# Expert products of a mixture layer: Strassen's seven products over pairs of hidden tiles and pairs of token blocks

## The chip, the cores and the metric

One core of one Trainium2 chip runs the whole program. The metric is device time in microseconds (us) of one execution. A core has TensorE (matmuls into eight PSUM banks of 128 x 512 floats), ScalarE (ACT), VectorE (DVE), GpSimd (POOL) and 16 DMA engines; SP issues most transfers. Each engine takes its instructions in the order in which they stand, and waits for others by semaphores.

## What is computed

Three layers, one after another. The middle one is a mixture of eight experts in which every token goes through every expert, weighted by a gate matrix P that Sinkhorn rounds balance:

```python
x = attention(q, k, v, beta)                 # 3072 tokens x 384
P = exp(x @ w_gate - max)                    # 3072 x 8
for _ in range(8):
    P /= P.sum(1, keepdims=True) + 1e-09
    P /= P.sum(0, keepdims=True) + 1e-09
    P *= N / E
for e in range(E):                           # E = 8, hidden size 1024
    h = np.maximum(x @ w1[e], 0.0)
    out += P[:, e:e + 1] * (h @ w2[e])
h = out @ w_in                               # hidden size 2048
return (h * np.cos(h)) @ w_out
```

## The kernel before, in words

Every operand of a matmul is kept as two parts, `hi` (its leading bits) and `lo` (the remainder), so that a product of two numbers is three matmuls: hi x hi, hi x lo, lo x hi. A token block is 512 tokens (there are six), a hidden tile 128 columns of `w1[e]` (eight per expert), and the model dimension 384 is three tiles of 128 (`KD = 3`). The first product of a hidden tile and a block is thus 3 x 3 = 9 matmuls of 128x128 by 128x512 (`h_mms`, line 132), followed by ReLU and split: ScalarE writes `hi` (line 159), VectorE the remainder `lo` (line 160). The second product is 9 matmuls into three banks (`yT_mms`, line 153), which sum over the expert's eight hidden tiles.

The program has these stages. While attention runs, expert 0 is worked through block by block in its gaps (`moe0_h`, `moe0_y`; `half()` takes the next piece); its results go to DRAM (`ysc`). The blocks of tokens, split, go to DRAM too (`xsc`). When attention's memory is closed, `begin_blocks` (line 802) loads all six blocks and six accumulators into SBUF, where they stay; expert 0's last block, the Sinkhorn rounds (`sk_some`, lines 583 to 621) and the first weights overlap. Then a single loop over experts 1 to 7, blocks and hidden tiles (line 1156) issues the first product of the next step, then the second product of this one. Once per expert and block, `moe_acc` multiplies the three banks by the gate (VectorE, line 1021) and adds them to the accumulator (GpSimd, line 1022). Weights are loaded once per expert, two hidden tiles at a time, and split by ScalarE and VectorE (`w_half`, lines 122 and 123). In the same loop, pieces of `conv` (lines 933 to 968) turn the 64-bit weights of the last layer into two floats on VectorE. `net_step` and `net_y` are the last layer; a rounding step of it (line 1064) and the splitting of its inputs are GpSimd's, as is the issuing of its weight loads (`w2_load`, lines 1043 and 1044).

```python
for i, (e, b, f) in enumerate(steps):
    if i + 1 < len(steps):
        moe_h(i + 1)
    ...
    moe_y(i)
    ...
    n = i // FT
    if n and 1 <= f <= 3:
        moe_acc(n - 1, f - 1)
```

Of the kernel before, what the change touches and what calls it, by code (L numbers as in the profile page):

```python
# [35 lines left out]
def kernel(  # L36
# [544 lines left out]

    def sk_max():
        nc.vector.tensor_reduce(out=mx, in_=logits.rearrange("p u e -> p (u e)"), axis=AX.X, op=ALU.max)

    def sk_max_t():
        nc.tensor.transpose(pa[3][0:1, 0:128], mx, ident)
        nc.vector.tensor_reduce(out=mr, in_=pa[3][0:1, 0:128], axis=AX.X, op=ALU.max)

    def sk_exp():
        nc.tensor.matmul(out=pa[3][:, 128:129], lhsT=ones[0:1, :], rhs=mr, start=True, stop=True)  # L590
        nc.vector.tensor_scalar(out=neg_mx, in0=pa[3][:, 128:129], scalar1=-1.0, scalar2=None, op0=ALU.mult)
        nc.scalar.activation(out=P, in_=logits, func=ACTF.Exp, bias=neg_mx)
        sk_rows()
# [17 lines left out]
    def sk_T():  # L611
# [29 lines left out]
    def moe0_y(s):  # L641
# [3 lines left out]
        if f == FT - 1:  # L645
            for kd in range(KD):
                if m in acc:
                    nc.scalar.activation(out=acc[m][:, kd, :], in_=yb[kd], func=ACTF.Copy)
                else:
                    y = ap2.tile([128, 512], F32, tag="y0", name="y0")  # L650
                    nc.scalar.activation(out=y, in_=yb[kd], func=ACTF.Copy)
                    nc.sync.dma_start(out=ysc[m][:, kd, :], in_=y)
                    stored.add(m)
# [8 lines left out]
    with tc.manual_schedule():  # L662
# [129 lines left out]
        xblk, xq, bigp, scr = {}, [], [], []  # L792

        def x_tile():
            return bigp[0].tile([128, 2, KD, 512], F32R, tag="x", name="x", bufs=NB)

        def load_block(b):
            nc.gpsimd.dma_start(out=xblk[b], in_=xsc[b])
            if b in stored:
                nc.sync.dma_start(out=acc[b], in_=ysc[b])  # L800

        def begin_blocks():

            att.close()
            bigp.append(ctx.enter_context(tc.tile_pool(name="big", bufs=1)))
            for b in range(NB):
                xblk[b] = x_tile()
            for b in range(NB):
                acc[b] = bigp[0].tile([128, KD, 512], F32, name=f"acc{b}")
            scr.append(hp.tile([128, 3072], F32, tag="xb", name="scr"))  # L810
            stage.append(scr[0][:, 1536:3072])

            w_load(NG + 1, scr[0][:, 0:1536])
            w_load(NG + 2)
            load_block(0)
            xq.extend(lambda b=b: load_block(b) for b in range(1, NB))

# [432 lines left out]
```

## Time and profile before

| what | value |
|---|---|
| median of 3 runs | 2257.78 us (2255.49 to 2258.95) |
| span of the profiled execution | 2254.0 us |
| TensorE busy | 2194.1 us |
| VectorE, ScalarE, GpSimd busy | 977.0, 627.2, 513.2 us |
| moved by DMA | 123.93 MB |

The profile is of one execution: from its first to its last instruction are 2254.0 us, 3.78 us less than the median of the runs, which is timed around the whole of it; the profile gives no other time for that execution. A busy engine may still wait inside an instruction: a matmul's time is from its start to its result, and matmuls follow each other faster than that, so their pace is read from the distance of their starts. PE stands for TensorE, PEld for its weight loads, "PEclk" for the share of full clock that it was granted. `<-` names what released an engine that had been idle.

### The profile page before, as it was taken

The numbers are of one execution on the slowest core, as the hardware profiler recorded it, in microseconds if no ns is written. First come the engines' busy times: TensorE is split into PE (matmuls) and PEld (weight loads), VectorE is DVE, ScalarE is ACT, GpSimd is POOL, SyncE is SP. The second block draws the span as 40 slices with busy tenths as digits, with TensorE's granted clock in tenths as the row PEclk, the third lists the DMA queues.
The fourth block names the chain that finished last, engine by engine and source line by source line (L and its number), as shares of the span: only waits on it lengthen the run. The fifth ranks groups of instructions, "written<-read, shape, count | busy, mean of one in ns | idle before, by whom it ended". The sixth has DMA issues, their size and how long they took to land.

```text
span 2254.0 us, 38564 instructions
## 1 busy us (share of the span) xinstructions
PE 2194.1 (97%) x16693; PEld 1837.2 (82%) x16693; DVE 977.0 (43%) x1591; ACT 627.2 (28%) x1017; POOL 513.2 (23%) x717
## 2 busy tenths in 40 slices
PE   6889999999999999999999999999999999999998
PEld 5677777788888888888888888888888878888887
DVE  6554543352343344334333433433322236666665
ACT  2233332321121122112112211211111135566665
POOL 4656544302210110111011101101111122222221
PEclk7889999999999999999999999999999999999999
DMA  4442321433131012112202210210112130000000
GB/s 83 101 94 66 80 66 52 180 102 104 44 84 47 26 49 80 28 30 80 52 23 58 70 32 26 80 52 27 43 37 65 38 113 2 14 15 15 15 15 15
DMA packets 167723, 123.93 MB, mean 55 GB/s; under 512 B 80272, under 2 KB 159664, under 8 KB 166784
## 3 DMA queue, kind: packets, MB, share of 16 engines
q1 hardware_dynamic: 161904, 97.26, 16.0%
q0 software_dynamic: 4480, 23.90, 3.1%
q8 instruction: 131, 2.15, 0.4%
q10 hardware_dynamic: 1168, 0.30, 0.1%
q14 instruction: 40, 0.33, 0.0%
HBM read 90.65 MB, written 30.77 MB: 54 GB/s over the span
## 4 chain that ended last, share of the span: by engine, by line
PE 92%; DVE 4%; ACT 2%; issue 1%; POOL 1%; DMA 0%; DVEq 0%; POOLq 0%; ACTq 0%
PE ps L132 43%; PE ps L153 34%; PE ps L142 8%; PE ps L281 1%; PE ps L467 1%; PE ps L255 1%; PE ps L437 1%; PE ps L449 1%; PE ps L495 1%; PE ps L510 0%; PE ps L542 0%; PE ps L525 0%; POOL kr L210 0%; DVE kr L246 0%; DVE xb L548 0%
## 5 line engine op out<-in xcount | busy, mean ns | idle before, releaser
L132 PE MATMUL ps<-x,w1t 128*128 128x512 f32 x3564 | 874.4, 390 | 0.0
L153 PE MATMUL ps<-h,w2t 128*128 128x512 f32 x3456 | 854.4, 392 | 0.0
L132 PEld LDWEIGHTS ps<-x,w1t 128*128 128x128 f32 x3564 | 668.0, 188 | 136.2
L153 PEld LDWEIGHTS ps<-h,w2t 128*128 128x128 f32 x3456 | 648.3, 189 | 135.1
L160 DVE SCALAR_TENSOR_TENSOR h<-ps,h 128x512 fp32r<-128x512 f32 x384 | 265.5, 691 | 945.4 <-ACT h L159 945.4
L159 ACT ACTIVATE h<-ps 128x512 fp32r<-128x512 f32 x384 | 229.5, 598 | 1229.9 <-PE ps L132 1229.9
L1022 POOL TENSOR_TENSOR acc<-acc,scr 128x512 f32<-128x512 f32 x126 | 166.1, 1318 | 1098.5 <-DVE scr L1021 1092.5
L142 PE MATMUL ps<-w2t,h 128*128 128x384 f32 x720 | 138.1, 338 | 5.0 <-DVE h L1088 2.1
L142 PEld LDWEIGHTS ps<-w2t,h 128*128 128x128 f32 x720 | 126.9, 188 | 14.5 <-DVE h L1088 4.5
L1078 DVE TENSOR_TENSOR tp<-tp,ps 128x512 f32<-128x512 f32 x96 | 66.0, 688 | 146.1 <-ACT tp L1077 146.1
L132 PE MATMUL ps<-xb,w1t 128*128 128x512 f32 x432 | 115.3, 410 | 6.1 <-ACT xb L547 2.7
L1064 POOL TENSOR_SCALAR tp<-tp 128x512 f32<-128x512 f32 x96 | 60.0, 625 | 256.5 <-ACT tp L1063 256.3
L132 PEld LDWEIGHTS ps<-xb,w1t 128*128 128x128 f32 x432 | 79.4, 192 | 26.4 <-DVE xb L548 3.5
L360 POOL TENSOR_TENSOR w1t<-w1t 128x30 f32<-128x30 f32 (+9 forms) x180 | 96.3, 535 | 14.1
L356 POOL TENSOR_TENSOR w1t<-Nsys,w1t 128x30 f32<-128x30 f32 (+9 forms) x180 | 90.4, 502 | 13.6
L1021 DVE TENSOR_TENSOR scr<-ps,scr 128x512 f32<-128x512 f32 x126 | 85.9, 682 | 8.6 <-DMA scr<-pts 5.6
L142 PE MATMUL ps<-x,h 128*128 128x384 f32 x432 | 83.5, 339 | 0.0
L1083 ACT ACTIVATE h<-tp 128x512 fp32r<-128x512 f32 x96 | 60.7, 632 | 76.9 <-DVE tp L1078 70.2
L132 PE MATMUL ps<-x 128*128 128x512 f32 x324 | 80.8, 393 | 1.3 <-DVE scr L1021 1.3
L1072 ACT ACTIVATE tp<-tp 128x512 f32<-128x512 f32 x96 | 60.7, 632 | 73.2 <-DVE tp L1069 73.2
L142 PEld LDWEIGHTS ps<-x,h 128*128 128x128 f32 x432 | 76.2, 188 | 5.7 <-DVE h L1088 2.5
L132 PEld LDWEIGHTS ps<-x 128*128 128x128 f32 x324 | 60.2, 188 | 12.7 <-DVE scr L1021 1.6
(187 smaller groups left out, 1411.0 us busy)
## 6 DMA issues: line engine op xcount, KB each, us to landing
scr<-in_moe_w_dram SPq DMA_DIRECT2D x54, 384.0 KB
scr<-pts SPq DMA_DIRECT2D x48, 256.0 KB
xsc<-xb SPq DMA_DIRECT2D x24, 384.0 KB
x<-xsc POOLq DMA_DIRECT2D x6, 1536.0 KB, 10.3
tp<-in_moe_w_in_dram SPq DMA_DIRECT2D x16, 384.0 KB
wsa<-tp SPq DMA_DIRECT2D x32, 192.0 KB
tp<-in_moe_w_out_dram SPq DMA_DIRECT2D x16, 384.0 KB
wsb<-tp SPq DMA_DIRECT2D x32, 192.0 KB
```

Source lines behind the costliest of these rows:

```text
L132: nc.tensor.matmul(out=ps[:, :nn], lhsT=w[:, a, kk, fs], rhs=x[:, b, kk, c0:c0 + nn], start=(i == 0), stop=(i == 3 * KD - 1),)
L142: nc.tensor.matmul(out=ps[:, :DM], lhsT=h[:, a, ts], rhs=w[:, b, f % 2, :], start=(first and i == 0), stop=(last and i == 2),)
L153: nc.tensor.matmul(out=banks[kd], lhsT=w[:, a, f % 2, kd * 128:(kd + 1) * 128], rhs=h[:, b, :], start=(first and b == 0 and a == 0), stop= ...
L159: nc.scalar.activation(out=h[:, 0, :nn], in_=ps[:, :nn], func=ACTF.Relu)
L160: nc.vector.scalar_tensor_tensor(out=h[:, 1, :nn], in0=ps[:, :nn], scalar=0.0, in1=h[:, 0, :nn].bitcast(F32), op0=ALU.max, op1=ALU.subtract,)
L356: eng.tensor_tensor(out=a, in0=nsys[:, j + 1:, j:j + 1].to_broadcast([128, n, j]), in1=xsys[:, j:j + 1, 0:j].to_broadcast([128, n, j]), op ...
L360: eng.tensor_tensor(out=xsys[:, j + 1:, 0:j], in0=xsys[:, j + 1:, 0:j], in1=a, op=ALU.add)
L1021: nc.vector.tensor_tensor(out=t, in0=ysets[n % 2][kd], in1=pb[e, b], op=ALU.mult)
L1022: nc.gpsimd.tensor_tensor(out=acc[b][:, kd, :], in0=acc[b][:, kd, :], in1=t, op=ALU.add)
L1072: nc.scalar.activation(out=rr[i % 2], in_=rr[i % 2], func=ACTF.Abs)
L1078: nc.vector.tensor_tensor(out=c, in0=c, in1=hb2(i), op=ALU.mult)
L1083: nc.scalar.activation(out=h[:, 0], in_=c, func=ACTF.Copy)
```

## The change

For experts 1 to 7 the loop is turned round: pairs of token blocks are the outer loop (three), then experts, then groups of two hidden tiles (four), 84 groups in all. In a group the first product is a 2 x 2 by 2 x 2 matrix of tiles (two model tiles by two hidden tiles, times two model tiles by two blocks), and is made by seven products of sums of tiles in the form of Strassen and Winograd, each of three matmuls. The third model tile is done so that its two cross terms (hi x lo and lo x hi, the smaller ones scaled by 4096) ride along as a fourth matmul in each of the seven (`c` and `T[:, 2, :]`), and its hi x hi is four single matmuls (`zz`). The results are put together in four PSUM banks (A, G, B, D) by copies from bank to bank on ScalarE and two additions on VectorE. Sums of tokens (`t_prep`) are made once per pair, kept in SBUF as `T0` to `T6`, and those of pairs 1 and 2 are written to DRAM (`tsc`) in the background and loaded at the change of pair. Sums of weights (`s_prep`) are made in every group, by GpSimd from the raw weights, which are loaded anew for each pair. The second product of two groups and one block is four pieces of nine matmuls (`seg_piece`), put between the seven products as fill (`F`); after four pieces the banks go through the gate (`gates`), twice per expert and block instead of once. Only two accumulators are in SBUF; finished ones go to DRAM (`xacc`) and come back for the last layer.

```diff
-        steps = [(e, b, f) for e in range(1, E) for b in range(NB) for f in range(FT)]
...
+        def mm(bank, n, i, start=False, stop=True):
+            h, l, c = s_hi(n, i), s_lo(n, i), s_c(n, i)
+            T = Tt[i]
+            for q, (a, b) in enumerate(((h, T[:, 0, :]), (h, T[:, 1, :]), (l, T[:, 0, :]), (c, T[:, 2, :]))):
+                nc.tensor.matmul(
+                    out=bank, lhsT=a, rhs=b, start=start and q == 0, stop=stop and q == 3, skip_group_check=True
+                )
+
+        def zz(bank, n, f, t):
+            nc.tensor.matmul(
+                out=bank, lhsT=s_z(n, f), rhs=Tt[(1, 6)[t]][:, 2, :], start=False, stop=True, skip_group_check=True
+            )
...
+        def seg_piece(m, q):
+
+            n = m // 2 * 2 + q // 2
+            h = hm_t.pop((n, q % 2, m % 2))
+            w2_t[-1] = W2[n]
+            yT_mms(yb, -1, q % 2, h, q == 0, q == 3)
+            if q == 3:
+                gq.append(m)
...
+        def gates():
+            while gq:
...
+                for kd in range(KD):
+                    c = ctile()
+                    nc.vector.tensor_tensor(out=c, in0=yb[kd], in1=pslot[t], op=ALU.mult)
+                    nc.gpsimd.tensor_tensor(out=accp[t][:, kd, :], in0=accp[t][:, kd, :], in1=c, op=ALU.add)
+                if j >= NG - 2:
+                    if e + 1 < E:
+                        p_load(t, e + 1, b)
+                    else:
+                        nc.sync.dma_start(out=xacc[b], in_=accp[t])
+                        if p + 1 < NP:
+                            acc_begin(p + 1, t)
+                            late.append(lambda p=p, t=t: acc_mul(p + 1, t))
...
+            s7, s4 = ctile(), ctile()
+            mm(A_, n, 0, True)
+            tl(0)
+            mm(G_, n, 5, True)
+            tl(5)
+            copy(B_, A_)
+            F()
+            gates()
+            if n >= 2:
+                fill.extend([lambda m=n - 2, q=q: seg_piece(m, q) for q in range(4)])
+            copy(s7, G_)
+            nx[0]()
+            mm(A_, n, 4)
+            tl(4)
+            copy(D_, A_)
+            mm(B_, n, 1)
+            zz(B_, n, 0, 0)
+            zz(G_, n, 1, 1)
+            skp(n)
+            nx[1]()
+            bg()
+            F()
+            mm(D_, n, 3)
+            tl(3)
+            mm(A_, n, 2)
+            zz(A_, n, 1, 0)
+            tl(2)
+            tl(1)
+            copy(s4, D_)
+            skp(n)
+            relu(n, 0, 0, B_)
+            nc.vector.tensor_tensor(out=s7, in0=A_, in1=s7, op=ALU.add)
+            nx[2]()
+            nx[3]()
+            nx[4]()
+            while late:
+                late.pop(0)()
+            F()
+            mm(D_, n, 6)
+            zz(D_, n, 0, 1)
+            tl(6)
+            skp(n)
+            nc.vector.tensor_tensor(out=s4, in0=G_, in1=s4, op=ALU.add)
+            relu(n, 1, 0, s7)
+            bg()
+            nx[5]()
+            if n + 2 < NGR:
+                g_load(n + 2)
+            relu(n, 1, 1, s4)
+            F()
+            relu(n, 0, 1, D_)
+            bg()
...
+        lead = [tq[0], tq[1], sq[0], tq[2], sq[1], sq[2], tq[3], sq[3], tq[4], sq[4], tq[5], sq[5], tq[6], tq[7]]
+        nb = 0
+        while len(mq) > 4:
+            half()
+            nb += 1
+            for _ in range(2):
+                if lead:
+                    lead.pop(0)()
+            if nb % 2 == 0:
+                sk_some()
+        for x in lead:
+            x()
+        g_load(1)
```

`nx` are the six pieces of `s_prep` for the next group: four sums on GpSimd, splits on ScalarE and VectorE, four more sums on GpSimd, and the split of `w2`. `bg` takes a piece of background work: first the token sums of pairs 1 and 2, then `conv`. `tl` loads the next pair's tiles in the last group of a pair, `skp` does one Sinkhorn round in groups 0 to 2, and `acc_mul` weights the reloaded sum of expert 0 by its gate. `tq` are the eight pieces of the token sums of the first pair, which stand beside what is left of expert 0 (`mq`).

**Order, TensorE in the middle of experts 1 to 7.** Before, one row is nine matmuls:

```order
L153 MATMUL ps8_98<-h_11448,w2t_10204 128x512 x9
L132 MATMUL ps8_98<-x_6345,w1t_11102 128x512 x9
L153 MATMUL ps8_98<-h_11471,w2t_11103 128x512 x9
L132 MATMUL ps8_98<-x_6345,w1t_11154 128x512 x9
L153 MATMUL ps8_98<-h_11494,w2t_11103 128x512 x9
L132 MATMUL ps8_98<-x_6345,w1t_11154 128x512 x9
```

In the change, most of one group; `T_6348` to `T_6354` are `T0` to `T6`, `mh` are hidden tiles, line 1179 is `mm`, 1184 `zz`, 155 the second product:

```order
L1179 MATMUL ps_107<-T_6348,w1t 128x512 x4
L1179 MATMUL ps_107<-T_6353,w1t 128x512 x4
L155 MATMUL ps_107<-mh,w2t 128x512 x9
L1179 MATMUL ps_107<-T_6352,w1t 128x512 x4
L1179 MATMUL ps_107<-T_6349,w1t 128x512 x4
L1184 MATMUL ps_107<-T_6349,w1t 128x512
L1184 MATMUL ps_107<-T_6354,w1t 128x512
L155 MATMUL ps_107<-mh,w2t 128x512 x9
L1179 MATMUL ps_107<-T_6351,w1t 128x512 x4
L1179 MATMUL ps_107<-T_6350,w1t 128x512 x4
L1184 MATMUL ps_107<-T_6349,w1t 128x512
L155 MATMUL ps_107<-mh,w2t 128x512 x9
```

First and second product no longer alternate nine by nine; not shown of this group are product 6 (four), its single matmul and a fourth nine of line 155; with them it is 32 matmuls of the first product and 36 of the second.

**Order, VectorE in the same place.** Before, a ReLU's remainder now and then stands beside conversion (lines 955 to 962) and gate products:

```order
L160 SCALAR_TENSOR_TENSOR h<-ps_98,h 128x512
L960 TENSOR_SCALAR tp<-tp 128x384
L961 SCALAR_TENSOR_TENSOR tp<-tp 128x384
L962 SCALAR_TENSOR_TENSOR tp<-tp 128x384
L160 SCALAR_TENSOR_TENSOR h<-ps_98,h 128x512 x2
L1021 TENSOR_TENSOR scr<-ps_98,scr 128x512
```

In the change, from the first hidden tile's remainder (line 162) on: the two sums of banks (1306 and 1317), the weights of the next group (976 to 989, and 1004) and conversion (1150 to 1152) stand in one row:

```order
L162 SCALAR_TENSOR_TENSOR mh<-ps_107,mh 128x512
L1306 TENSOR_TENSOR ct<-ps_107,ct 128x512
L976 TENSOR_TENSOR w1t<-scr,w1t 128x128
L977 TENSOR_TENSOR w1t<-scr,w1t 128x256
L981 SCALAR_TENSOR_TENSOR w1t<-scr,w1t 128x256
L989 TENSOR_TENSOR w1t<-ct,w1t 128x512
L1317 TENSOR_TENSOR ct<-ps_107,ct 128x512
L162 SCALAR_TENSOR_TENSOR mh<-ct,mh 128x512
L1150 TENSOR_SCALAR tp<-tp 128x384
L1151 SCALAR_TENSOR_TENSOR tp<-tp 128x384
L1152 SCALAR_TENSOR_TENSOR tp<-tp 128x384
L1004 TENSOR_TENSOR w2t<-scr,w2t 128x768
```

Work that was spread over four steps now stands between the end of one product and the next gate products.

**Order, ScalarE at the end of attention**, with what each waits for. Before (159 is ReLU of expert 0, 122 the weights, 592 the exponential of the gates):

```order
L122 ACTIVATE w1t<-stg 128x768 [waits Pool_49]
L122 ACTIVATE w2t<-stg 128x768 [waits Activation_49]
L159 ACTIVATE h<-ps_98 128x512 [waits DVE_49,PE_49] x2
L122 ACTIVATE w1t<-scr 128x768 [waits DMAHW6_49]
L122 ACTIVATE w2t<-scr 128x768 [waits DMAHW7_49]
L592 ACT_TABLE_LOAD [waits DVE_49]
L592 ACTIVATE P<-logits,small 128x192 [waits Activation_49]
L159 ACTIVATE h<-ps_98 128x512 [waits PE_49,Activation_49] x2
```

In the change, the splits of token sums (1034, 1082) and the sums of weights (965 to 988, 1003) stand between the ReLUs (161):

```order
L161 ACTIVATE h<-ps_107 128x512 [waits DVE_49,PE_49]
L1034 ACTIVATE T_6351<-mh 128x512 [waits DVE_49]
L965 ACTIVATE w1t<-scr 128x128 [waits DMAHW4_49,Pool_49]
L966 ACTIVATE w1t<-scr 128x256
L968 ACTIVATE w1t<-scr 128x256
L969 ACTIVATE w1t<-w1t 128x256 [waits Activation_49]
L161 ACTIVATE h<-ps_107 128x512 [waits PE_49]
L1034 ACTIVATE T_6353<-mh 128x512 [waits DVE_49]
L988 ACTIVATE w1t<-ct 128x512 [waits Pool_49]
L1034 ACTIVATE T_6352<-mh 128x512 [waits DVE_49]
L161 ACTIVATE h<-ps_107 128x512 [waits PE_49]
L1034 ACTIVATE T_6350<-mh 128x512 [waits DVE_49]
```

The ReLUs of expert 0's last block, on which TensorE waits, now stand behind instructions that wait for VectorE, GpSimd and DMA.

## Rows read from the trace of the kernel before

**Rows 1.** The page: busy us, share of the span and instructions of each engine.

```profile
PE 2194.1 (97%) x16693; PEld 1837.2 (82%) x16693; DVE 977.0 (43%) x1591; ACT 627.2 (28%) x1017; POOL 513.2 (23%) x717
```

**Rows 2.** Busy time by stretch; columns PE, PEld, DVE, ACT, POOL, then PEclk, DMA share, GB/s.

```profile
560.00:1792.00 1232.00, 1232.00 (x5437) 1020.15 (x5436) 444.80 (x744) 215.90 (x351) 169.68 (x128) 1.00 0.17 49
```

**Rows 3.** Timeline of two steps: start us, us, instruction [idle before <- releaser].

```profile
1001.45 2.20 PE L153 MATMUL ps<-h,w2t 128*128 128x512 f32 x9
...
1001.64 0.60 ACT L159 ACTIVATE h<-ps 128x512 fp32r<-128x512 f32 x1 [3.48 <-PE ps L132]
...
1002.27 0.69 DVE L160 SCALAR_TENSOR_TENSOR h<-ps,h 128x512 fp32r<-128x512 f32 x1 [2.79 <-ACT h L159]
...
1003.49 2.20 PE L132 MATMUL ps<-x,w1t 128*128 128x512 f32 x9
```

**Rows 4.** Groups of instructions with shapes: busy us, mean ns, idle before.

```profile
L1022 POOL TENSOR_TENSOR acc<-acc,scr 128x512 f32<-128x512 f32 x126 | 166.1, 1318 | 1098.5 <-DVE scr L1021 1092.5 <-issue 6.0
...
L1021 DVE TENSOR_TENSOR scr<-ps,scr 128x512 f32<-128x512 f32 x126 | 85.9, 682 | 8.6 <-DMA scr<-pts 5.6 <-POOL acc L1022 2.8
...
L123 DVE TENSOR_TENSOR w1t<-scr,w1t 128x768 fp32r<-128x768 f32 x27 | 25.8, 957 | 1.9 <-ACT w1t L122 1.1
...
L952 DVE SCALAR_TENSOR_TENSOR tp<-tp 128x384 f32<-128x384 f32 x32 | 17.9, 559 | 1.1
...
L957 DVE TENSOR_SCALAR tp<-tp 128x384 int32<-128x384 int32 x32 | 11.5, 360 | 1.1
...
L356 POOL TENSOR_TENSOR w1t<-Nsys,w1t 128x130 f32<-128x130 f32 x12 | 5.2, 431 | 0.9
```

**Rows 5.** Timeline at 640 us: VectorE and GpSimd.

```profile
640.36 0.95 DVE L123 TENSOR_TENSOR w1t<-scr,w1t 128x768 fp32r<-128x768 f32 x1
...
640.52 1.93 POOL L1022 TENSOR_TENSOR acc<-acc,scr 128x512 f32<-128x512 f32 x1 [2.73 <-DVE scr L1021]
...
641.23 2.04 DVE L123 TENSOR_TENSOR w2t<-scr,w2t 128x768 fp32r<-128x768 f32 x1
```

**Rows 6.** Timeline and TensorE's waits, expert 0's last block.

```profile
429.14 0.39 SPq L105 DMA_DIRECT2D scr<-in_moe_w_dram  x1
...
436.49 2.33 PE L132 MATMUL ps<-xb,w1t 128*128 128x512 f32 x9
...
446.31 0.15 DVE L604 TENSOR_SCALAR small<-ps 128x8 f32<-128x8 f32 x1
...
448.67 0.53 DVE L600 TENSOR_REDUCE small<-P 128x8 f32<-128x192 f32 x1
...
PE ps L603 <- DVE small L600: 0.3, 1, 0.3
```

**Rows 7.** Busy time by stretch, while blocks are loaded; the last column is GB/s.

```profile
430.00:432.00 2.00, 2.00 (x11) 1.68 (x11) 1.23 (x2) 1.67 (x3) 0.00 (x0) 1.00 0.91 284
...
440.00:442.00 2.00, 2.00 (x10) 1.43 (x9) 1.96 (x4) 0.92 (x2) 0.00 (x0) 1.00 1.08 436
```

**Rows 8.** Busy time by stretch around a pause of TensorE.

```profile
308.00:312.00 4.00, 2.83 (x13) 1.80 (x11) 2.57 (x2) 1.11 (x3) 0.00 (x0) 1.00 0.30 112
312.00:316.00 4.00, 4.00 (x138) 3.78 (x139) 3.41 (x3) 1.31 (x4) 0.89 (x1) 0.92 0.19 70
316.00:320.00 4.00, 4.00 (x68) 2.96 (x69) 0.00 (x0) 1.13 (x2) 3.31 (x11) 0.66 0.51 97
```

**Rows 9.** Timeline of TensorE and GpSimd at the turn to the net.

```profile
1841.34 1.51 PE L142 MATMUL ps<-w2t,h 128*128 128x384 f32 x7 [0.65 <-DVE h L1088]
...
1844.03 0.80 PE L142 MATMUL ps<-w2t,h 128*128 128x384 f32 x3 [1.18 <-DVE scr L1021]
...
1846.11 2.35 PE L132 MATMUL ps<-x 128*128 128x512 f32 x9 [1.28 <-DVE scr L1021]
...
1850.12 2.00 PE L142 MATMUL ps<-w2t,h 128*128 128x384 f32 x10 [1.32 <-DVE h L1088]
...
1812.71 0.55 POOL L1043 DMA_DIRECT2D w1t<-wsa  x1
```

More of the change, by code (lines that the diff above doesn't have):

```diff
@@ L627, in sk_some @@
             sk.pop(0)()
-    h0_t, acc, stored = {}, {}, set()
+    h0_t, tmp2 = {}, [lambda: ap2.tile([128, 512], F32, tag="y0", name="y0")]
     def moe0_h(s):
         m, f = divmod(s, FT)
-        bank = pa[0] if scr and s % 2 else hb
+        bank = pa[0] if scr and s % 2 and not grp else hb
         h_mms(bank, f // 2, f, xb[m], 0, 512)
@@ L646, in moe0_y @@
             for kd in range(KD):
[L647 to L653, printed above, removed]
+                y = tmp2[-1]()
+                nc.scalar.activation(out=y, in_=yb[kd], func=ACTF.Copy)
+                nc.sync.dma_start(out=ysc[m][:, kd, :], in_=y)
     NS0 = NB * FT
@@ L789 @@
         nc.scalar.activation(out=wg[:, :, 0, :], in_=wg_sb, func=ACTF.Copy)
[L792 to L816, printed above, removed]
+        scr, grp = [], []
         mq = [(2, lambda: moe0_h(0))]
@@ new lines, with F, bg, skp @@
+        fill = []
+        def F():
+            if fill:
+                fill.pop(0)()
+        bgq = []
+        def bg(k=1):
+            for _ in range(k):
+                if bgq:
+                    bgq.pop(0)()
+        def skp(n):
+            if n <= 2 and sk:
+                sk_some()
+                if not sk:
+                    for t in range(2):
+                        acc_begin(0, t)
+                        late.append(lambda t=t: acc_mul(0, t))
+        def group(n):
+            p, e, j = gidx(n)
+            swap = e == E - 1 and j == NG - 1 and p + 1 < NP
+            nx = s_prep(n + 1) if n + 1 < NGR else [lambda: None] * 6
+            def tl(i):
+                if swap:
+                    t_load(p + 1, i)
+            s7, s4 = ctile(), ctile()
[50 more added lines that the diff above has]
+            bg()
@@ L1207 @@
-        w2_load(7)
-        for kd in (0, 2, 1):
-            moe_acc(len(steps) // FT - 1, kd)
+        grp.append(1)
+        skb[0] = hb
+        for bank in (B_, D_):
+            nc.tensor.matmul(
+                out=bank, lhsT=s_hi(0, 0), rhs=Tt[0][:, 0, :], start=True, stop=True, skip_group_check=True
+            )
+        fill.extend(lambda: half() for _ in range(len(mq)))
+        group(0)
+        assert not fill and not mq
+        tpv = tpt.rearrange("p a (s c) -> p (a s) c", c=512)
```

374 lines of the change are left out of this document (263 added, 111 removed).

## The prediction

> **What bounds the kernel now.** I read the page's busy times first: TensorE is busy 97% of the span, twice any other engine [rows 1]. I then cut the span by stage. In the stage of experts 1 to 7 the engine has no idle time at all: 1232.00 of 1232.00 us busy at clock 1.00 [rows 2]. So this stage is worth what its matmuls take, one after another, and nothing else. Their pace comes from the timeline: nine matmuls of the second product start at 1001.45, the next nine at 1003.49 [rows 3]: 2.04 us for nine, 0.2267 us each (the 0.39 us that the profile gives one matmul is its latency, not its pace). The 336 steps of 18 matmuls make 6048 x 0.2267 = 1371 us, from about 448 to 1811 us. The other engines have slack: per step of 4.08 us ScalarE works 0.60 and waits 3.48, VectorE 0.69 and mostly waits [rows 3].
>
> **What the change takes away.** One group (two hidden tiles, two token blocks) had 2 x 2 x 9 = 36 matmuls in the first product. Now it has seven products of four, and four single ones: 32. The second product keeps its 36. All are 128x128 by 128x512 as before, so I price them at the same pace. There are 7 experts x 4 x 3 pairs = 84 groups: 84 x 4 x 0.2267 = **76.2 us less**. Two added matmuls that only prime banks cost 0.5 us.
>
> **One group laid out in time.** The 68 matmuls take 15.4 us if nothing waits. From the order of the change: product 0 ends at 0.9, product 5 at 1.8, nine of the second product (I call nine such a filler) at 3.85, then products 4 and 1 and two single ones to 6.1, filler to 8.2, products 3 and 2 and a single to 10.2, filler to 12.2, product 6 and a single to 13.4, filler to 15.4. Results are readable some 0.2 us later.
> ScalarE (0.60 us each for 512 columns [rows 4]; a copy from bank to bank has no row, and I take the same; its bounds are 0.4 and 1.2, and neither reaches a wait): copy A to B at 1.1, needed at 4.8; copy of G at 2.0, needed at 5.9; copy A to D at 4.95, needed at 8.2; four weight pieces to 7.1; copy of D at 9.3, needed at 12.2. Every one is 2 us early or more.
> GpSimd: three gate additions of 1.32, then eight weight sums of 128x128. The nearest row is 128x130, 0.43 [rows 4]: 4.0 + 3.4 = 7.4 of 15.4 us.
> VectorE is the tight one. It makes three gate products of 0.68 [rows 4] from 4.05 to 6.1; TensorE's next filler overwrites their banks one by one from 6.1 on. Then it waits behind ScalarE's copy of D and the first ReLU until 10.5. From there in order: remainder of the first hidden tile 0.69 [rows 3], sum 0.68, three weight remainders (my estimate 1.15 in all, scaled from 0.96 for 768 columns [rows 4]), one of 512 columns 0.69, sum 0.68, remainder 0.69, weights of the second product 0.96, two remainders 1.38: it ends at 17.4. In every second group three conversion operations (0.56 twice and 0.36 [rows 4]) make it 18.9. The next gate products can start at 15.4 + 3.85 + 0.2 = 19.4, and TensorE wants the first of them at 15.4 + 6.1 = 21.5, so the chain may end at 20.8: 1.9 us to spare with a conversion, 3.4 without.
> What eats into that is seen at 640 us [rows 5]: GpSimd's addition, started during VectorE's 0.95 us subtraction of two SBUF tiles, took 1.93 instead of 1.29, and VectorE's next one, started under it, 2.04 instead of 0.95. The second to start waits for the first. The change puts five such VectorE operations and four GpSimd sums in the same 4 us. Taking turns with pieces of 0.43 puts 0.8 to 1.7 on VectorE's chain: with a conversion it ends at 19.7 to 20.6. Still before 20.8, by little; without one, 1.7 to 2.6 us are left.
> [...]
> **Steady term: +8 us**, 0 to 20. About 4 for the sums of tokens of pairs 1 and 2, which sit on ScalarE, VectorE and GpSimd beside groups 2 to 11, some ten pieces of which push a bank copy past its time by about 0.4; 4 for conversion groups at the edge. Below nothing it can't be.
>
> **Weights and tokens by DMA.** Weights are now read and split three times (84 loads of 768 KB, 66 MB for 22). One takes 786 KB / 284 GB/s = 2.8 us [rows 7], and I allow 5 for issue and landing. It is issued when VectorE has read the old ones (13 to 16.5) and first needed 5.5 us into the next group (20.9), and 4 us later than that ScalarE's delay would reach product 6. Hidden by the matmuls; each microsecond beyond would be one per group. At the two changes of pair 5.5 MB of token tiles go through: at 436 GB/s [rows 7] 13 us, at 284 19. Tile 1 is issued at 10.3 and wanted at 20.2, tile 6 at 13.4 and 21.3. I take **+1 us**, 0 to 10. The store and reload of the two accumulators holds up SP and GpSimd, so the next weights land 9 us into a group; product 6's cover of 12.2 holds.
>
> **The start** is where the gain goes. Before, expert 0's last block (420 to 463 us) ran beside weight splits and the Sinkhorn rounds, and TensorE's matmuls waited 0.3 us for those [rows 6]. Now the token sums for the first pair stand there too, on ScalarE ahead of the ReLUs and on VectorE ahead of the maximum, on whose transpose TensorE waits in order. I walked the order with the rows' durations:
> - 3.7 MB are queued ahead of the first sum. They can start at 429 as the weights do now [rows 6], and at 284 to 436 GB/s [rows 7] land near 439; two additions of 1.32, subtraction, copy, remainder, and the maximum is out at 443. TensorE has run out at 438.4, nine matmuls later than those of 436.49 start [rows 6]: **4.7**, then **1.0** at the next small matmul.
> - the first Sinkhorn round waits for two more sums, the weights of group 0, the table load: **5.5**; the next stands behind four corrections of 0.69: **3.0**, and 0.5 inside group 0.
> - group 1 has no filler yet (32 matmuls, 7.3 us), while VectorE has some 10 us of its own and up to three Sinkhorn rounds of 2.9 [rows 6]: product 5 waits 4.0 for a bank, product 4 2.7 for ScalarE, 2.6 more: **9.3**. Group 2 in the same way **4.2**.
> Sum **+28 us**. Bounds: the 0.3 of before, and 45 if nothing of it overlaps.
> Pauses also cost clock: the row from 308 has TensorE idle 1.2 us, and in the next 8 us the granted clock is 0.92 and 0.66, a mix of 1.2 and 2.4 GHz [rows 8]: (0.08 + 0.34) x 4 = 1.7 us lost. Some eight pauses above 1 us would lose 14; part falls into time that is waited anyway. **+6 us**, 2 to 14.
>
> **The end.** Before, TensorE idles 4.4 us at the turn to the last net [rows 9]. Now the last accumulator must be stored before GpSimd may issue the load into its place, and ten issues of 0.55 [rows 9] stand ahead of the third rounding step: additions 5.0, store 4, issues 5.5, against 11 us of ready matmuls. I get 8 us idle: **+4 us**, 0 to 8. The net itself keeps its order and its pace.
>
> **Sum:** -76.2 + 0.5 + 28 + 6 + 4 + 8 + 1 = -28.7. The profiled span of 2254.0 becomes 2225.3; the median of the runs shown is 3.8 above that span, and so **2229 us**. A measurement of this kernel can tell about 0.2% (4.5 us) from no change.
>
> **Rivals.**
> 1. *The start overlaps better.* The transfers land at 400 GB/s and more [rows 7], the pauses shrink to 12 and their clock to 3: 2229 - 19 = **2210**. For: DMA did 436 just there. Against: in-order queues.
> 2. *Conversion groups overrun.* If each GpSimd sum also waits its full turn, VectorE ends 0.5 us too late in some 40 groups: 20 us: **2249**. For: [rows 5]. Against: the chain still has 0.2 to 1.1 us left. The part above 2253 I count as same.
> 3. *Slower: VectorE becomes the bound of every group.* Its chain from 10.5 needs only 3 us more than I have, from waiting its turn at every operation with two SBUF inputs and from hand-overs between engines. From 0.35 us of TensorE wait per group on the gain is gone (29 / 84). One us each is 84 - 8 more: **2305**. Against: plain groups keep some 2 us. For: no stretch of the profile runs VectorE and GpSimd this densely on each other's tiles.
> 4. *The matmuls are not saved*: they are counted in the order, so I give it nothing.
>
> **How the numbers follow.** Forecast 0.55 (2213 to 2245), rival 1 0.17, rival 2 0.16 (0.10 faster, 0.06 same), rival 3 0.12. Faster 0.55 + 0.17 + 0.10 = 0.82, same 0.06, slower 0.12. Range: below, start and end at their low bounds, about 2198; above, start, clock and steady terms high, 2260. It leaves out rival 3.
>
> **What would show it.** Right: in the middle of the stage 68 matmuls per 15.4 us with TensorE busy throughout; idle TensorE of some 28 us between 436 and 505, waiting for VectorE in lines of the Sinkhorn matmuls and of groups 1 and 2; the granted clock below 1 there; a gap of about 8 us at the turn to the net. Wrong: TensorE waits for VectorE's gate products in every group; subtractions of 512 columns at 1 us and more in the mean; bank copies late; the weights' DMA named as a releaser.

## The result, and the profile after

The change made the kernel 1.0% slower: median 2282.38 us of 4 runs (2277.26 to 2283.63) against 2258.36 us, ratio 1.0101 (95% interval 1.0086 to 1.0115). The forecast was 2229 us, faster than before. The profiled execution has a span of 2279.6 us. The page's busy times, as in [rows 1]:

```profile
PE 2170.4 (95%) x16359; PEld 1787.7 (78%) x16359; DVE 1439.6 (63%) x2285; ACT 994.4 (44%) x1819; POOL 1090.8 (48%) x1521
```

TensorE works 24 us less than before and yet the span is 26 us longer. Where that is, busy time by stretch shows (columns as in [rows 2]; the x behind a busy time counts instructions, matmuls in the first column). After: expert 0's last block and groups 0 to 4, groups 5 to 29, the first change of pair, groups 33 to 57, the second change with the groups around it, groups up to the last, last group and net:

```profile
419.95:566.82 146.87, 115.12 (x452) 88.03 (x450) 85.58 (x168) 52.11 (x103) 53.31 (x64) 0.90 0.39 130
566.82:961.83 395.01, 394.60 (x1702) 319.06 (x1700) 281.83 (x447) 184.78 (x362) 225.70 (x280) 1.00 0.37 116
961.83:1019.38 57.55, 50.78 (x206) 40.35 (x205) 34.08 (x54) 21.34 (x42) 32.66 (x35) 0.94 0.39 128
1019.38:1413.71 394.33, 394.33 (x1702) 319.19 (x1700) 289.38 (x466) 179.28 (x350) 218.12 (x276) 1.00 0.32 99
1413.71:1482.86 69.15, 65.51 (x273) 51.61 (x272) 48.76 (x75) 28.53 (x56) 41.76 (x46) 0.98 0.36 117
1482.86:1814.10 331.24, 331.24 (x1429) 268.09 (x1428) 223.10 (x360) 149.88 (x294) 182.42 (x231) 1.00 0.25 77
1814.10:2279.57 465.47, 442.63 (x2166) 391.82 (x2164) 268.25 (x418) 253.04 (x423) 110.84 (x150) 0.98 0.15 51
```

Before, the two stretches that stand beside the first and the last of these:

```profile
419.45:560.00 140.55, 138.72 (x620) 112.41 (x618) 58.80 (x132) 33.12 (x54) 21.43 (x15) 1.00 0.42 148
...
1792.00:2254.00 462.00, 449.27 (x2201) 396.87 (x2200) 265.98 (x413) 252.52 (x422) 95.13 (x132) 1.00 0.08 25
```

Three things are to be seen. **The groups run without a gap**, as forecast: 394.33 of 394.33 us busy at clock 1.00. But a stretch of 394.33 us holds 1702 matmuls, 0.2317 us each, where [rows 2] give 1232.00 / 5437 = 0.2266. **The start** takes 146.87 us for 452 matmuls, 35 of them the small ones of gates and Sinkhorn rounds, at clock 0.90; 417 x 0.2267 = 94.5 are 52.3 us short of it. Before, 140.55 us hold 620, also 35 small: 7.9 short. So the start lost 44.4 us. **The changes of pair** and **the end** have pauses: 57.55 - 50.78 = 6.8 us at the first change, 69.15 - 65.51 = 3.6 at the second, both with the clock below 1 behind them. The end is 3.5 us longer than before with 35 matmuls fewer (7.9 us): 11.4 us lost.

What TensorE waited for, over the whole span (us in total, times, longest):

```profile
PE ps L144 <- DVE h L1391: 14.9, 1, 14.9
...
PE ps L1179 <- ACT ct L1189: 12.1, 4, 3.5
PE ps L590 <- DVE small L587: 8.7, 1, 8.7
PE ps L607 <- DVE small L604: 5.8, 4, 3.3
PE ps L155 <- DVE ct L1233: 5.0, 3, 3.7
```

And in the timeline of a group, beside [rows 3]:

```profile
704.13 2.24 PE L155 MATMUL ps<-mh,w2t 128*128 128x512 f32 x9
706.21 1.10 PE L1179 MATMUL ps<-T,w1t 128*128 128x512 f32 x4
```

Nine of the second product now start 2.08 us before the next matmul (704.13 to 706.21), where [rows 3] have 2.04. Nothing is named as a releaser: a pause of a few ns inside every matmul has no row of its own.

| term of the sum | forecast, us | measured, us |
|---|---|---|
| 336 matmuls fewer, two more | -75.7 | -75.7 |
| pace of the groups: 84 x (15.77 - 15.41) | 0 | +30 |
| start, with its clock (44.4 less 1.8 of pace) | +34 | +43 |
| sums and conversion inside groups | +8 | +1 |
| changes of pair, with their clock | +1 | +16 |
| end (11.4 less one group's pace) | +4 | +11 |
| sum; the span moved by +25.6 | -28.7 | +25 |

15.77 us is the distance of one group's first matmul to the next one's, the same for 72 of the 83 distances to 0.01 us. The pair term is what five groups at the two changes took beyond 15.77 us each (5.3, 4.9, 4.3, 1.7 and 0.1 us).

### The profile page after: what moved, and what is told of

It reads as the page before. It is cut to its first block, busy times and chain, and to the rows that moved or that the text cites. A ratio compares the mean times of both kernels' runs of the same rounds, so it can differ in the third digit from the quotient of the medians.

```text
span 2279.6 us, 40883 instructions
## 1 busy us (share of the span) xinstructions
PE 2170.4 (95%) x16359; PEld 1787.7 (78%) x16359; DVE 1439.6 (63%) x2285; ACT 994.4 (44%) x1819; POOL 1090.8 (48%) x1521
## 4 chain that ended last, share of the span: by engine, by line
PE 85%; DVE 5%; DMA 4%; ACT 2%; issue 2%; POOL 2%; SPq 1%; POOLq 0%; DVEq 0%; ACTq 0%
PE ps L155 32%; PE ps L1179 22%; PE ps L134 12%; PE ps L144 8%; PE ps L1184 3%; PE ps L283 1%; PE ps L257 1%; DMA accp<-ysc 1%; PE ps L469 1%; DMA xacc<-accp 1%; DMA scr<-in_moe_w_dram 1%; PE ps L451 1%; PE ps L439 1%; POOL accp L1234 1%; POOL accp L1220 1%
## 5 line engine op out<-in xcount | busy, mean ns | idle before, releaser
L155 PE MATMUL ps<-mh,w2t 128*128 128x512 f32 x3024 | 754.1, 394 | 5.0 <-DVE ct L1233 5.0
L155 PEld LDWEIGHTS ps<-mh,w2t 128*128 128x128 f32 x3024 | 569.7, 189 | 140.3 <-DVE ct L1233 7.5
L1179 PE MATMUL ps<-T,w1t 128*128 128x512 f32 x2352 | 613.4, 400 | 21.5 <-ACT ct L1189 12.1
L1179 PEld LDWEIGHTS ps<-T,w1t 128*128 128x128 f32 x2352 | 445.0, 190 | 130.5 <-ACT ct L1189 14.2
L1234 POOL TENSOR_TENSOR accp<-accp,ct 128x512 f32<-128x512 f32 x252 | 334.9, 1356 | 326.6 <-DVE ct L1233 326.6
L162 DVE SCALAR_TENSOR_TENSOR mh<-ps,mh 128x512 fp32r<-128x512 f32 x168 | 115.1, 685 | 311.8 <-ACT mh L161 311.8
L1189 ACT ACTIVATE ps<-ps 128x512 f32<-128x512 f32 x168 | 97.8, 582 | 324.7 <-PE ps L1179 313.9
L1233 DVE TENSOR_TENSOR ct<-ps,scr 128x512 f32<-128x512 f32 x252 | 158.3, 683 | 76.4 <-PE ps L155 73.7
L1189 ACT ACTIVATE ct<-ps 128x512 f32<-128x512 f32 x168 | 100.3, 597 | 219.7 <-PE ps L1179 214.3
L161 ACT ACTIVATE mh<-ct 128x512 fp32r<-128x512 f32 x168 | 106.2, 633 | 131.6 <-DVE ct L1306 71.2
L144 PE MATMUL ps<-w2t,h 128*128 128x384 f32 x720 | 138.6, 340 | 16.5 <-DVE h L1391 14.9
L162 DVE SCALAR_TENSOR_TENSOR mh<-ct,mh 128x512 fp32r<-128x512 f32 x168 | 144.1, 858 | 0.1
L1184 PE MATMUL ps<-T,w1t 128*128 128x512 f32 x336 | 119.8, 397 | 0.0
L155 PE MATMUL ps<-h,w2t 128*128 128x512 f32 x432 | 117.8, 420 | 0.0
```

Source lines behind the costliest of these rows:

```text
L144: nc.tensor.matmul(out=ps[:, :DM], lhsT=h[:, a, ts], rhs=w[:, b, f % 2, :], start=(first and i == 0), stop=(last and i == 2),)
L155: nc.tensor.matmul(out=banks[kd], lhsT=w[:, a, f % 2, kd * 128:(kd + 1) * 128], rhs=h[:, b, :], start=(first and b == 0 and a == 0), stop= ...
L161: nc.scalar.activation(out=h[:, 0, :nn], in_=ps[:, :nn], func=ACTF.Relu)
L162: nc.vector.scalar_tensor_tensor(out=h[:, 1, :nn], in0=ps[:, :nn], scalar=0.0, in1=h[:, 0, :nn].bitcast(F32), op0=ALU.max, op1=ALU.subtract,)
L1179: nc.tensor.matmul(out=bank, lhsT=a, rhs=b, start=start and q == 0, stop=stop and q == 3, skip_group_check=True)
L1184: nc.tensor.matmul(out=bank, lhsT=s_z(n, f), rhs=Tt[(1, 6)[t]][:, 2, :], start=False, stop=True, skip_group_check=True)
```

## The experiments

Theories at the outset: the pace is lost to the **addresses** of the token tiles, or (rival) to the **density** of the other engines' accesses; the pauses come from what stands ahead in **in-order queues**, or (rival) from the **transfers and work** themselves, in any order.

### The pace: where the tiles start

The allocator puts `T0` to `T6` at the upper end of SBUF; `T0` starts at byte 186,336 of each partition, 32 past a multiple of 64. All operands of the large matmuls before (`x`, `h`, weights) start at multiples of 64. These addresses stand in no row of a trace; they are read from the built programs. Experiment 1 adds 32 bytes to that pool, so that `T0` starts at byte 186,304, a multiple of 64, and to that of the net, whose weights lay the same way:

```diff
         Tt = [tpool.tile([128, 3, 512], F32R, name=f"T{i}") for i in range(7)]
+        tpool.tile([128, 8], F32, name="pad")
```

> Theory (address): the token tiles T0 to T6 start 32 bytes past a multiple of 64, every tile that TensorE streamed before at a multiple of 64, and this costs some of each matmul's pace. With 32 bytes more in the pool all tiles lie at multiples of 64: a group should fall from 15.77 us to 15.41 (68 x 0.2267), 84 x 0.36 = 30 us less, about 2252 us (2247 to 2257). Rival (density: the many reads and writes of the other engines slow the matmuls): nothing changes, 15.77 us per group and 2278 to 2286 us.

Measured: 2254.16 us, ratio to before 0.9983 (0.9974 to 0.9992). Experiments 2 and 8 go the other way, in the kernel before: `x` moved by 32 bytes, then the weights alone (the second tile brings what lies behind back to a multiple of 64).

```diff
+            bigp[0].tile([128, 8], F32, name="pad")
             for b in range(NB):
                 xblk[b] = x_tile()
+            bigp[0].tile([128, 8], F32, name="pad2")
...
     hp = ctx.enter_context(tc.tile_pool(name="hp", bufs=2))
+    wp.tile([128, 8], F32, tag="pad", name="pad", bufs=1)
+    hp.tile([128, 8], F32, tag="pad", name="pad2", bufs=1)
```

> The kernel before, with only its blocks of tokens moved by 32 bytes. Theory (address): 9 of the 18 matmuls of a step read such a tile. The changed kernel lost 0.36 us in 68 matmuls of which 32 do; in proportion a step of 4.08 us grows by about 0.1, 336 steps by some 33 us: about 2291 us (2275 to 2305). Rival (density): the other engines do the same as before, so no change, 2254 to 2262 us.

> The kernel before, with only its weight tiles moved by 32 bytes (read by TensorE as the stationary operand, and as the streamed one in 720 matmuls of the last layer); tokens and hidden tiles stay. If only the streamed operand's address counts: no change beyond some 3 us in the last layer, 2254 to 2264 us. If the stationary one counts as much: 33 us and more, 2285 to 2330 us.

Measured: 2288.03 us, ratio 1.0133 (1.0118 to 1.0148), and 2299.97 us, 1.0181 (1.0166 to 1.0196). The duration of a matmul of line 1179 (first product) and 155 (second) between 1019 and 1414 us, as min/median/max in ns; first the changed kernel:

```profile
L1179 PE MATMUL ps<-T,w1t x700: 393/397/400, 1019.4 to 1411.2; 128*128 128x512 f32 x175
...
L155 PE MATMUL ps<-mh,w2t x901: 387/393/403, 1019.1 to 1413.5; 128*128 128x512 f32 x181
```

Experiment 1 (its line 1180 is `mm`; the maxima are matmuls right behind a pause that ends at 1411 us, at its second change of pair), and its busy time by stretch:

```profile
L1180 PE MATMUL ps<-T,w1t x706: 388/390/794, 1019.1 to 1412.3; 128*128 128x512 f32 x177
...
L155 PE MATMUL ps<-mh,w2t x911: 388/390/629, 1019.8 to 1413.6; 128*128 128x512 f32 x183
```

```profile
1020.00:1400.00 380.00, 380.00 (x1678) 314.85 (x1677) 285.96 (x461) 176.57 (x344) 213.73 (x270) 1.00 0.32 102
```

380.00 us hold 1678 matmuls: 0.2265 us each, the old pace with all the new density around it. Experiment 2 (line 132 first, 153 second product) and, in the stretch of [rows 2], experiments 2 and 8:

```profile
L132 PE MATMUL ps<-x,w1t x846: 392/396/400, 1021.1 to 1411.7; 128*128 128x512 f32 x170
...
L153 PE MATMUL ps<-h,w2t x853: 388/394/398, 1019.2 to 1413.5; 128*128 128x512 f32 x171
```

```profile
560.00:1792.00 1232.00, 1232.00 (x5307) 997.22 (x5306) 441.32 (x737) 210.68 (x342) 163.85 (x122) 1.00 0.17 48
```

```profile
560.00:1792.00 1232.00, 1232.00 (x5281) 989.67 (x5280) 438.51 (x738) 210.25 (x341) 160.53 (x119) 1.00 0.16 47
```

With 5437 in the same 1232.00 us before, the pace went from 0.2266 to 0.2321 and 0.2333 us, while the other engines did what they had always done. So the address decides, in both kernels and for the streamed and the stationary operand alike. The second product was slowed in experiment 2 too (394), though its own tiles had not moved: it alternates with matmuls that were slowed. How a delay passes on was not tried; nor were offsets other than 32.

### The changes of pair

> The changed kernel with one transfer issue (the gate row of expert 1, which waits for GpSimd's weighting of the reloaded accumulator) moved behind the weights of the next group in the queue. Theory (queue): at both changes of pair TensorE waits because the weights are issued behind that wait; 16 us were lost at the two changes, 3 should stay: about 2269 us (2264 to 2274), and no pause of over 1 us at the changes. Rival (transfers: 5.5 MB at each change take the time that they take): the pauses stay, 2278 to 2286 us.

```diff
-            p_load(t, 1, b)
+            late2.append(lambda t=t, b=b: p_load(t, 1, b))
...
                 g_load(n + 2)
+            while late2:
+                late2.pop(0)()
```

Measured: 2276.73 us, 1.0079 (1.0064 to 1.0095), a gain of under 6 us where 13 were expected. The queue in the changed kernel, first SP's timeline, then ScalarE's:

```profile
954.78 0.34 SPq L1239 DMA_DIRECT2D xacc<-accp  x1
...
958.60 0.33 SPq L1216 DMA_DIRECT2D accp<-ysc  x1
968.12 0.36 SPq L1208 DMA_DIRECT2D scr<-pts  x1
...
969.66 0.48 SPq L924 DMA_DIRECT2D scr<-in_moe_w_dram  x1
...
976.07 0.31 ACT L965 ACTIVATE w1t<-scr 128x128 fp32r<-128x128 f32 x1 [8.57 <-DMA scr<-in_moe_w_dram]
...
977.34 0.58 ACT L1189 ACTIVATE ct<-ps 128x512 f32<-128x512 f32 x1
```

SP loads the new accumulator at 958.60, then stands until 968.12, when GpSimd has weighted it, for the gate row; only then come the weights (969.66). They reach ScalarE at 976.07. Its copy of bank D, due in this group, stands behind them in its queue (977.34), and that is the row `L1179 <- ACT ct L1189`. In experiment 3 the longest pauses at the two changes fell to 1.4 and 1.2 us, as the theory had it, but one elsewhere grew, in group 3:

```profile
PE ps L155 <- DVE ct L1233: 15.4, 1, 15.4
```

The edit had moved the row for the first pair too, where group 3 needs it at once (3.7 us there before). Experiment 6 moves it for pairs 1 and 2 alone (`if p:` ahead of the new line, the old one else), on top of experiment 5:

> The one before, with the gate row of expert 1 issued behind the next group's weights, for pairs 1 and 2 alone (the third experiment had moved it for pair 0 too). Theory (queue): the two changes of pair lose 16 us, of which 3 stay: 13 us less than the one before, about 2230 us (2225 to 2235). Rival (transfers): under 4 us less than the one before.

Measured: 2245.35 us, 0.9937 (0.9921 to 0.9954), 12.4 us less than experiment 5. At the first change TensorE then waits 0.3 us for a token tile, and this:

```profile
PE ps L1181 <- DVE ct L1322: 1.3, 1, 1.3
```

### The end

> The changed kernel with the last layer's weight loads issued by SP instead of GpSimd. Theory (queue): GpSimd's rounding step stands behind ten issues that wait for the store of the accumulator; without them it runs at 1859.4 instead of 1872.4, TensorE's pause of 15 us becomes about 2, and of the 13.7 us at half clock behind it most goes: about 2266 us (2261 to 2271). Rival (weights late): the pause moves to the first hidden tile whose weights are loaded there and less than 5 us are gained, 2277 to 2285 us.

```diff
-            nc.gpsimd.dma_start(out=a, in_=wsa[g])
-            nc.gpsimd.dma_start(out=c, in_=wsb[g])
+            nc.sync.dma_start(out=a.bitcast(F32), in_=wsa[g])
+            nc.sync.dma_start(out=c.bitcast(F32), in_=wsb[g])
```

Measured: 2283.02 us, 1.0113 (1.0096 to 1.0130): no gain. GpSimd in the changed kernel, its last additions, the first of ten issues, and the rounding step:

```profile
1855.61 3.79 POOL L1234 TENSOR_TENSOR accp<-accp,ct 128x512 f32<-128x512 f32 x3 [4.74 <-DVE ct L1233]
1864.06 0.57 POOL L1346 DMA_DIRECT2D xw<-wsa  x1 [4.66 <-DMA xacc<-accp]
...
1872.38 0.63 POOL L1367 TENSOR_SCALAR tp<-tp 128x512 f32<-128x512 f32 x1
```

The issues stand from 1859.4 to 1872.4 ahead of the rounding: 4.7 us until the accumulator is stored, ten issues of 0.55, and 2.9 us ahead of the ninth and the tenth. In experiment 4 that pause is down to 1.9 us, but a new one takes its place (TensorE's waits, then ScalarE's timeline):

```profile
PE ps L144 <- ACT h L1386: 12.8, 1, 12.8
```

```profile
1883.40 0.63 ACT L1332 ACTIVATE xx<-nacc 128x512 fp32r<-128x512 f32 x1 [14.02 <-DMA nacc<-xacc]
```

The next accumulator's load had stood ahead of the weights on SP and now stood behind 7.9 MB of them (ten loads of 768 KB). Experiment 7 puts it first again, on top of experiment 6:

```diff
+        x2_load(1)
         for g in range(3, 8):
             w2_load(g)
-        x2_load(1)
```

> The one before, with the last layer's weight loads on SP's queue and the load of the second accumulator ahead of them (in the fourth experiment it stood behind them, and TensorE waited 13 us for it). Theory (queue order): the pause of 15 us falls to about 2 and of its 13.7 us at half clock most goes: 14 us less than the one before, about 2216 us (2210 to 2222). Rival (transfers): 7.7 MB of weights are late in any order, the pause moves again, under 5 us less than the one before.

Measured: 2229.60 us, 0.9875 (0.9859 to 0.9891), 15.8 us less than experiment 6, and 29 us less than the kernel before in the same runs. TensorE's wait at this place:

```profile
PE ps L144 <- DVE h L1398: 1.9, 1, 1.9
```

### The start

Line 587 is the maximum whose transpose TensorE awaits. In the changed kernel it ran at 447.36, behind a token sum that waited for GpSimd, which waited for a load (GpSimd, then VectorE):

```profile
442.06 1.26 POOL L1051 TENSOR_TENSOR mh<-mh 128x512 f32<-128x512 f32 x1 [29.58 <-DMA mh<-xsc]
```

```profile
444.83 0.93 DVE L1056 TENSOR_TENSOR mh<-mh 128x512 f32<-128x512 f32 x1 [8.40 <-POOL mh L1052]
...
447.36 0.34 DVE L587 TENSOR_REDUCE small<-logits 128x1 f32<-128x192 f32 x1
```

Experiment 5 loads those four tiles ahead of 2.6 MB of others, on top of experiment 1 (`tq` is counted from the second piece on then).

```diff
+        tq.pop(0)()
         g_load(0)
...
-        lead = [tq[0], tq[1], sq[0], tq[2], sq[1], sq[2], tq[3], sq[3], tq[4], sq[4], tq[5], sq[5], tq[6], tq[7]]
+        lead = [tq[0], sq[0], tq[1], sq[1], sq[2], tq[2], sq[3], tq[3], sq[4], tq[4], sq[5], tq[5], tq[6]]
```

> Tiles at multiples of 64 (first of these experiments), and the four loads of the first token sum moved ahead of 2.5 MB of other transfers at the end of attention. Theory (order of the loads): the pause of 8.9 us before the transpose of the maximum and the 3.5 us after it come from those loads landing at 442; they land at about 434 then, the two pauses and the half clock behind them shrink by 9 to 14 us together: about 2243 us (2238 to 2247). Rival (engines): additions and splits of the sums take the time whenever they start, the pauses move to the next Sinkhorn rounds: 2250 to 2257 us.

Measured: 2257.76 us, 0.9996 (0.9984 to 1.0008): no gain over experiment 1. GpSimd's sums in it, and TensorE's waits from 421 to 600 us:

```profile
431.04 1.29 POOL L1052 TENSOR_TENSOR mh<-mh 128x512 f32<-128x512 f32 x1 [22.48 <-DMA mh<-xsc]
...
440.86 1.27 POOL L1059 TENSOR_TENSOR mh<-mh 128x512 f32<-128x512 f32 x1 [4.69 <-DMA mh<-xsc]
```

```profile
PE ps L607 <- DVE small L604: 7.0, 3, 4.5
PE ps L594 <- DVE small L591: 6.2, 1, 6.2
...
PE ps L590 <- DVE small L587: 1.9, 1, 1.9
```

The first sum starts 11 us earlier and the wait at line 590 falls from 8.7 to 1.9 us, but the second and third sums wait for loads of their own (4.7 and 4.9 us), and lines 594 and 607 wait instead: the pauses moved, as the rival had it, here with loads behind them. Two experiments, 9 and 10, left work out, to see what the start consists of: the first has `range(2)` for `range(8)` in the list of Sinkhorn pieces, the second empty pieces in `tq`, and loads in place of the sums:

```diff
+        tq = [lambda: None] * 8
...
+        for i in (2, 3, 4, 5):
+            nc.sync.dma_start(out=Tt[i].bitcast(F32), in_=xsc[1].rearrange("p a k c -> p (a k) c")[:, 0:3, :])
```

> The seventh experiment (all corrections, 2229.6 us), with six of the eight Sinkhorn rounds left out. It still loses 47 us between attention and the sixth group. Theory (chain): the Sinkhorn rounds, one after another through TensorE and VectorE, set the end of the start; 15 us or more less, 2208 to 2216 us. Rival (token sums): the sums for the first pair set it, less than 5 us less, 2224 to 2232 us.

> The seventh experiment with the token sums of the first pair left out: unsummed tokens are loaded in their place, 3.5 MB as the operands of the sums were. Theory (token sums): the pauses of 7.1 and 5.4 us ahead of the first group go, and the half clock behind them: 10 to 15 us less, 2214 to 2220 us. Rival (chain of Sinkhorn rounds): less than 5 us less, 2224 to 2232 us.

Measured: 2217.67 us, 0.9823 (0.9794 to 0.9853), and 2211.69 us, 0.9796 (0.9772 to 0.9820): 12 and 18 us less than experiment 7, the first between its two forecasts, the second beyond both. Neither theory holds alone. Without the sums, group 0 begins at 451 instead of 471 us. With two Sinkhorn rounds another pause grows in the place of the rounds, 12.6 us for a copy that stands behind a weight load on ScalarE:

```profile
PE ps L1181 <- ACT ct L1191: 12.6, 1, 12.6
```

So leaving out the sums is worth more than leaving out six of the rounds; how the two add up was not tried. The eleventh experiment loads all their operands first, into six hidden tiles instead of three:

```diff
+            if direct:
...
+                for i, u in enumerate(use):
+                    pre[u] = sl(i)
+                    nc.sync.dma_start(out=pre[u], in_=xs(*u))
```

> The seventh experiment with all twelve loads for the first pair's sums issued at the start, into tiles of their own, ahead of the other transfers. There a second and a third sum waited on GpSimd for a load (5.3 and 4.8 us) that was issued only when the first ones were done. Theory (loads one behind the other): those waits go, 6 to 12 us less, 2217 to 2224 us. Rival (order of VectorE and the Sinkhorn rounds): the pauses move once more, less than 4 us less, 2226 to 2232 us.

Measured: 2227.45 us, 0.9868 (0.9844 to 0.9891), 2 us less than experiment 7, as its rival had it. The wait at line 594 was 8.9 us, and GpSimd stood with the second sum (447.79) behind weights that were late now:

```profile
PE ps L594 <- DVE small L591: 8.9, 1, 8.9
```

```profile
445.63 0.46 POOL L959 TENSOR_TENSOR ct<-scr 128x128 f32<-128x128 f32 x1 [5.02 <-DMA scr<-in_moe_w_dram]
...
447.79 1.25 POOL L1070 TENSOR_TENSOR mh<-mh 128x512 f32<-128x512 f32 x1
```

The twelfth orders the pieces as `lead = tq + sq` and calls `sk_some()` ahead of the two pieces of a turn, not behind them:

> The eleventh experiment (all twelve loads first, 2227.5 us), with the weights of the first group prepared behind all token sums instead of between them, and each Sinkhorn piece written ahead of the two pieces of sums that follow it. There GpSimd waited 5.0 us and ScalarE 3.7 for those weights in front of the second sum, and the reduction that the exponential needs stood behind three sums. Theory (in-order queues): the pause of 9.0 us falls to about 2, 6 to 10 us less with the clock, 2217 to 2222 us. Rival (work): the additions, splits and Sinkhorn pieces need the time in any order, 2224 to 2231 us.

Measured: 2217.26 us of 5 runs, 0.9822 (0.9809 to 0.9835). TensorE's longest wait from 421 to 600 us, which is for a gate product in group 3, and the one at line 594:

```profile
PE ps L155 <- DVE ct L1249: 5.0, 1, 5.0
...
PE ps L594 <- DVE small L591: 3.8, 1, 3.8
```

The time lies within the theory's range and outside the rival's: the order of the queues was a cost. Which of the two moves took it back was not tried. This version computes all that the reference does, is 39 us faster than the kernel before, and some 65 faster than the change as it was made. From attention's end to group 5 it takes 139.8 us, the changed kernel 146.87: most of the start's loss is still there, and what more of it could go was not tried.

## Why the prediction was wrong

**The saving was right.** 336 matmuls fewer at 0.2267 us are worth 76 us, and with aligned tiles the groups run at 15.41 us, the 68 matmuls of the prediction.

**"All are 128x128 by 128x512 as before, so I price them at the same pace" failed.** A matmul took 0.2317 us in the groups, not 0.2267. The prediction took the pace for a property of shape and type. The trace of before could not show otherwise, since every large tile in it lay at a multiple of 64; the layout of the changed program could, and the prediction did not look at it. This term alone, +30 us where the sum has none, turns the sum of -28.7 to about zero.

**VectorE's chain held, and its price was too high.** Gate products were late three times in all (`L155 <- DVE ct L1233`, 5.0 us): 3.7 us in the start, 0.9 at the second change of pair and 0.4 at the end, never in the groups between. (ScalarE's 0.60 us, for which the prediction names [rows 4], stands in [rows 3].) The turns between VectorE and GpSimd are there: two conversion steps of 128x384, in the group view (busy us, mean ns of one),

```profile
L1146 DVE SCALAR_TENSOR_TENSOR tp<-tp 128x384 int32<-128x384 int32 x13 | 20.0, 1538 | 0.4
L1147 DVE TENSOR_SCALAR tp<-tp 128x384 int32<-128x384 int32 x13 | 17.3, 1334 | 0.4
```

take 1538 and 1334 ns; before, steps of the same two kinds and size took 559 and 360 ([rows 4]). In all 13 cases of each, a gate addition of GpSimd (line 1234) was running when the step began, and the step ended 0.2 to 0.4 us after that addition; the other seven conversion steps, which met a shorter rest of GpSimd's work or none, took 344 to 699 ns. So what [rows 5] show at 640 us comes back in this stage. Line 1147 has a single SBUF input, and the prediction counted only operations with two. The Trainium skill ("SBUF — State Buffer", section "Who interferes with whom") counts such operations among those that can take the shared ports in a faster mode, and this row agrees. Rivals 2 and 3 made this delay TensorE's, but the chain's slack took it all: +1 us, not +8. Rival 3, the only slower one, had the sign right for a cause that did not occur.

**The changes of pair: +16, not +1.** The prediction had the weights "land 9 us into a group" and counted product 6 as the first to need them. They reached ScalarE 14 us into it (961.83 to 976.07), because a gate row waited ahead of them on SP; and the first to suffer was not the product that reads them but ScalarE's copy for the current group behind their split.

**The start: +43, not +34.** TensorE idled 31.75 us here (146.87 - 115.12) against 1.83 before, so the pauses cost 29.9 us, near the 28 of the forecast, but not where it had them. The one at the maximum was 8.7 us, not 4.7: the four loads were issued from 434.65 on, behind 2.6 MB, and the sum began at 442, not 439. The other pauses ahead of group 0 were shorter than forecast (4.1 us against 9.5), and those of groups 1 and 2 summed to 8.9 us against 13.5. But groups 3 and 4 had 8.3 more that the prediction did not list (3.7 us of `L155 <- DVE ct L1233`, and 2.7 and 2.0 of `L1179`). That their sum came out is luck, since these errors cancel. The term that was mis-sized is the clock: 42.6 us less 29.9 of pauses leave 12.7 for slower matmuls, at a granted clock of 0.90 in the mean of this stretch, where the forecast had 6.

**The end: +11, not +4.** The order of causes was right (additions, store, issues, rounding). 14.9 us instead of 8 came of 13 us between the additions and the rounding, 3.5 more than counted, 2.9 of it ahead of the last two issues; and the matmuls that were ready beside it lasted 6.5 us (1853.7 to 1860.2), not 11. The clock fell with the pause: 0.76 in the mean of 1856 to 1884 us.

The three errors that experiments 1, 6 and 7 took back bring the time to 2229.6 us, with experiment 5's order of loads, which gained nothing by itself. That it meets the forecast's figure is chance: the start's extra cost is still in it, and the end and the groups are cheaper than forecast.

## What to carry to other kernels

When a change moves operands of matmuls into new tiles, look where the tiles start: here 32 bytes past a multiple of 64 cost 2.3% of the matmuls' pace in a stage that does nothing else, which no wait shows; compare the matmul starts per us, not the busy shares. When an instruction must wait, list what stands behind it on its engine's queue for the *current* work, not only who needs its result. A queue corrected alone may move the wait to the next one: experiment 4 gained nothing until the load behind was put right as well, and experiment 5's load only moved the pause to the sums behind it.

## What the runs showed that was not expected

- The start address of an operand had a price in TensorE's pace in the stage of the experts: 0.2266 us per matmul with all operands at multiples of 64, 0.2317 with the tokens of the first product 32 past, 0.2333 with all weights 32 past. The Trainium skill ("SBUF — State Buffer", section "Operand start alignment") asks only for a multiple of the element's size, and says that this is about legality, not speed; the runs agree with the first (they ran at 32 past a multiple of 64) and add a price to the second.
- In the net, where matmuls of 512 and 384 columns alternate, the same 32 bytes cost nothing that can be seen. From 2000 to 2200 us, before and in experiment 8:

```profile
2000.00:2200.00 200.00, 199.07 (x990) 177.82 (x989) 125.37 (x196) 120.65 (x203) 41.94 (x59) 1.00 0.05 13
```

```profile
2000.00:2200.00 200.00, 198.68 (x990) 177.31 (x989) 125.20 (x196) 120.57 (x203) 41.18 (x58) 1.00 0.05 13
```

Both hold 990 matmuls. A matmul of the first product with 512 columns took 393 ns there in the kernel before already, with all operands at multiples of 64, as in the slowed groups; why was not looked into.
- A pause costs clock behind it. Behind the pause of 14.9 us at the end, which ended at 1875.11, TensorE was busy throughout, but 4 us held 15 matmuls at a granted clock of 0.60, a mix of its two levels of 1.2 and 2.4 GHz, and the next 4 us 22:

```profile
1876.00:1880.00 4.00, 4.00 (x15) 3.74 (x14) 2.58 (x4) 1.48 (x3) 0.30 (x1) 0.60 1.10 419
1880.00:1884.00 4.00, 4.00 (x22) 3.65 (x21) 1.58 (x3) 1.84 (x3) 0.62 (x1) 1.00 1.12 419
```
